# Attention in turns of four units: second pair's exponential bank by bank, and a first pair of banks that stays in place

## The chip, the core and the metric

The kernel runs on one core of one Trainium2 chip. The metric is the device time in microseconds (us). Before the change it is 1071.54 us, the median of 3 runs (1071.03 to 1071.62).

## What is computed

One token sequence of 2048 rows with 448 features goes through two blocks, and a sigmoid gate mixes their results. Everything is float32.

```python
g = sigmoid((x * gate_w).sum(-1, keepdims=True))
a = attention(x, wqkv, wo)        # 16 heads of 28, softmax over 2048 keys
b = mlp(layernorm(x), w1, b1, w2, b2)   # 448 -> 1792 (gelu) -> 448
return g * a + (1 - g) * b
```

The softmax subtracts the maximum of each row of the scores. The kernel gets it by a pass of its own: TensorE multiplies q and k once more, VectorE reduces each result to its maximum.

## The kernel before, in words

The kernel has two stages. In the first (to about 449.6 us) the projections and the MLP run, from an order that a planner made with costs in Python. In the second, which the change is in, attention runs in **turns** (`turn_of`, line 1147), one after another, with an order written out in the loop at line 1195.

The 16 heads form 4 groups of 4, and the queries 4 blocks of 512, so there are 16 rounds. A round has 64 **units**: a unit is the score block of one head, 128 keys by 512 queries, and needs one PSUM bank (128 partitions x 512 float32). `score` (line 1132) makes it in three matmuls, parts 0, 1 and 2, of which each uses one strip of 32 rows of TensorE; head j sits in strip j, and four strips work side by side. `soften` (line 1141) takes the exponential on ScalarE from PSUM into an SBUF tile (`p0` for the first pair, `p1` for the second). `batch` (line 1185) multiplies the four exponentials of a turn with the values, in 4 matmuls over 128 rows that add up in bank 7 (`pv`).

A turn of four units goes so: units 0 and 1 are the **first pair** (strips 0 and 1), units 2 and 3 the **second pair** (strips 2 and 3). TensorE's queue holds, in this order, a row-maximum matmul for strip 2 or 3 into bank 6 (`lone(behind, 6, turn)`, called L-behind below), the first pair's part 0, its part 1 with the second pair's part 0, its part 2 with the second pair's part 1, the second pair's part 2, then a row-maximum matmul for strip 0 or 1 (`lone(ahead, spare, turn)`, called L-ahead) and the four value matmuls of the turn before. ScalarE takes the first pair's exponential (both banks in one instruction, 128x1024) and then the second pair's (the same). VectorE reduces the results of L-behind and L-ahead (line 214, 128x512 to 128x1).

The banks: 0 to 5 form three pairs, (4,5), (2,3), (0,1), in this order in the list `pairs` (line 941 sorts them by the time at which the planner expects them free). A turn uses one for its first pair, one for its second, and the third is the **spare**, into whose first bank L-ahead writes. Line 1163 rotates them: a turn's spare is the next turn's first pair, and a turn's first pair is the next turn's second. So what stands in a bank must be gone before the next user writes: L-ahead waits for the exponential of the second pair of the turn before (the same banks), the next turn's first pair waits for VectorE's reduction of L-ahead, and the next turn's second pair waits for this turn's first exponential.

Row-maximum matmuls are left until about 978 us (`rowmax.left()`); then turns take seven units in banks 0 to 6, except near the output projections (`project`, line 1011, 12 matmuls through bank 6), where they stay at four.

Of the kernel before, what the change touches and what calls it, by code (L numbers as in the profile page):

```python
# [9 lines left out]
AF = mybir.ActivationFunctionType  # L10
# [19 lines left out]
SCALE = DH ** -0.5  # L30
# [5 lines left out]
def kernel(ctx: ExitStack, tc: tile.TileContext, xt, wqk, wv, wo, xk, w1, b1, w2, b2,  # L36
                          ident_d, sel_d, out):
    nc = tc.nc
# [35 lines left out]
    bk = banks.tile([P, 8, CH], F32, name="bk")  # L74
# [162 lines left out]
    rowmax = RowMax()  # L237
# [671 lines left out]
    for b, m in enumerate((0, 3, 4)):  # L909
        x = QK(0, m)  # L910
# [30 lines left out]
    pairs = sorted((0, 2, 4), key=lambda b: max(strips.free[b], strips.free[b + 1]))  # L941
# [134 lines left out]
    def begun(n, turn):  # L1076

        g, c = divmod(n, NC)
        if n + 1 < NG * NC:
            for j in range(4):  # L1080
                at(turn + 1 + j // 2, lambda j=j: fetch_qq(n + 1, j))
            at(turn + 7, lambda: split_qq(n + 1))
            at(turn + 10, lambda: load_ms(n + 1))
        if c == (0 if g == 0 else 2) and g < NG - 1:
            for j in range(4):
                at(turn + 2 + j, lambda j=j: fetch_kk(g + 1, j))
                at(turn + 10 + 2 * j, lambda j=j: split_kk(g + 1, j))
            at(turn + 18, lambda: key_row(g + 1))
            for t in range(2):
                at(turn + 12 + t, lambda t=t: load_v(g + 1, slice(8 * t, 8 * t + 8)))  # L1090
        if g == NG - 1:
            for i in range(TPC):
                at(turn + (8 if rowmax.left() else 7) + i, lambda i=i: fetch_acc(c, i))
                at(turn + (10 if rowmax.left() else 9) + i // 2, lambda i=i: weigh_acc(c, i))
            for x in range(NG - 1):
                at(turn + 4 + 2 * x, lambda x=x: split_o(x, c, ot[x][:, c * CH:(c + 1) * CH]))
# [21 lines left out]
    def lone(strips, b, turn):  # L1118
        s = min((s for s in strips if rowmax.ready(s) and turn >= cold[s]), key=lambda s: rowmax.cnt[s], default=None)
        if s is None:  # L1120
            return
        for kind, n, j in rowmax.one(s, bk[:, b]):
            if kind == "q":
                at(turn + 1, lambda n=n, j=j: rowmax.load_q(n, j))
            elif kind == "k":
                at(turn + 1, lambda n=n, j=j: rowmax.load_k(n, j))
                cold[j] = turn + 7
            else:
                at(turn + 1, lambda n=n: rowmax.close(n))
                at(turn + 2, lambda n=n: rowmax.store(n))  # L1130

    def score(x, p, b):
        n, k = divmod(x, 64)
        k, j = divmod(k, 4)
        r = slice(32 * j, 32 * j + DH + (p == 0))
        ks = slice(k * P, (k + 1) * P)
        w = (khi, klo, khi)[p][n // NC]
        q = (qh, qh, ql)[p][n % 3]
        nc.tensor.matmul(bk[:, b], w[r, ks], q[r], start=(p == 0), stop=(p == 2), skip_group_check=True)  # L1139

    def soften(u, half, b, count):
        t = ap.tile([P, 4 - half, CH], F32, name=f"p{half}")
        nc.scalar.activation(t[:, :count], bk[:, b:b + count], AF.Exp, scale=SCALE)  # L1143
        for i in range(count):
            prob[u + i] = t[:, i]

    def turn_of(u, turn):

        left = UNITS - u
        size = min(left, 7 if not rowmax.left() and not (tail and tail[0][0] <= turn + 1) else 4)  # L1150
        for x in range(u, u + size):
            n = x // 64
            if n not in begins:
                begins.add(n)
                begun(n, turn)
        if size > 4:
            for half, first, count in ((0, 0, 4), (1, 4, size - 4)):
                for p in range(3):
                    for i in range(first, first + count):
                        score(u + i, p, i)  # L1160
                soften(u + first, half, first, count)
            return size
        first, second, spare = (pairs[(2 * turn + i) % 3] for i in (0, 1, 2))
        na = min(size, 2)
        nb = size - na
        ahead = [(u + i) % 4 for i in range(2)]
        behind = [(u + i) % 4 for i in range(2, 4)]
        if rowmax.left() and turn not in projected:
            lone(behind, 6, turn)
        for step in range(4):  # L1170
            for i in range(na):
                if step < 3:
                    score(u + i, step, first + i)
            for i in range(nb):
                if step > 0:
                    score(u + 2 + i, step - 1, second + i)
            if step == 2:
                soften(u, 0, first, na)
        if nb:
            soften(u + 2, 1, second, nb)  # L1180
        if rowmax.left():
            lone(ahead, spare, turn)
        return size
# [11 lines left out]
    u = b = turn = 0  # L1195
    begun_half = False
    while b < UNITS // 4:
        before, quota = u, 99
        if u < UNITS:
            u += turn_of(u, turn)  # L1200
            if u - before > 5:
                quota = 3 + (before // 4 - b > 2)
                quota += 2 * (NT - b % NT) - begun_half == quota + 1
        for fn in agenda.pop(turn, ()):
            fn()
        if turn == 0:
            idle(6, 7)
        if before == UNITS:
            products(bk[:, 3, :D], (NC - 1) * TPC, range(NG - 1))
            before = u = UNITS  # L1210
        while 4 * b + 4 <= before and quota:
            if quota == 1 and not begun_half:
                if b % NT:
                    batch(b, turn, slice(0, CH // 2))
                    begun_half = True
                break
            last = batch(b, turn, slice(CH // 2 if begun_half else 0, CH))
            quota -= 1 if begun_half else 2
            b, begun_half = b + 1, False
            if last:  # L1220
                break
        if tail and tail[0][0] <= turn:
            project(tail.pop(0)[1])
            projected.add(turn + 1)
        turn += 1
# [53 lines left out]
```

## Time and profile before

| what | value |
|---|---|
| median of 3 runs | 1071.54 us |
| the profiled execution | 1071.13 us, of which the span from first to last instruction is 1069.3 us |
| TensorE busy | 1058.5 us (99%) |
| ScalarE busy | 647.6 us (61%) |
| VectorE busy | 749.8 us (70%) |
| GpSimd busy | 368.9 us (34%) |
| mean granted TensorE clock | 0.999 |

PE is TensorE's matmuls, PEld its weight loads (a matmul's waits stand at its weight load), ACT is ScalarE, DVE VectorE, POOL GpSimd, SP the engine that issues most DMAs. A row of the timeline has the start in us, the time from the first start to the last end of the merged instructions, engine, line, operation, result and operands, count, and in brackets how long the engine had been idle and what released it.

### The profile page before, as it was taken

The numbers are of one execution on the slowest core, as the hardware profiler recorded it, in microseconds if no ns is written. First come the engines' busy times: TensorE is split into PE (matmuls) and PEld (weight loads), VectorE is DVE, ScalarE is ACT, GpSimd is POOL, SyncE is SP. The second block draws the span as 40 slices with busy tenths as digits, with TensorE's granted clock in tenths as the row PEclk, the third lists the DMA queues.
The fourth block names the chain that finished last, engine by engine and source line by source line (L and its number), as shares of the span: only waits on it lengthen the run. The fifth ranks groups of instructions, "written<-read, shape, count | busy, mean of one in ns | idle before, by whom it ended". The sixth has DMA issues, their size and how long they took to land. (4 is left out here: it accounts for less than half of the span.)

```text
span 1069.3 us, 30804 instructions
## 1 busy us (share of the span) xinstructions
PE 1058.5 (99%) x13202; PEld 713.8 (67%) x13202; DVE 749.8 (70%) x1182; ACT 647.6 (61%) x773; POOL 368.9 (34%) x392
## 2 busy tenths in 40 slices
PE   9999999999999999999999999999999999999997
PEld 7999999999999999844444444444444444455455
DVE  4899998999999999866666665466666666634102
ACT  5234364033043033288888888888888888857762
POOL 5565578335344036451011101310111125363432
PEclk9999999999999999999999999999999999999999
DMA  7696443212100105230101101400002102121111
GB/s 236 217 272 216 169 106 97 86 55 61 38 13 10 37 16 124 75 90 22 30 2 23 28 13 31 116 22 17 15 21 64 51 12 55 29 62 47 45 54 61
DMA packets 47785, 73.18 MB, mean 68 GB/s; under 512 B 13840, under 2 KB 28816, under 8 KB 46848
## 3 DMA queue, kind: packets, MB, share of 16 engines
q1 hardware_dynamic: 33888, 39.11, 13.4%
q0 software_dynamic: 5120, 16.89, 5.8%
q10 hardware_dynamic: 8640, 15.21, 3.9%
q8 instruction: 103, 1.69, 0.7%
q14 instruction: 34, 0.28, 0.1%
HBM read 51.75 MB, written 19.31 MB: 66 GB/s over the span
## 5 line engine op out<-in xcount | busy, mean ns | idle before, releaser
L214 DVE TENSOR_REDUCE mx<-bk 128x1 f32<-128x512 f32 x1024 | 683.9, 690 | 209.6 <-PE bk L212 194.6
L1143 ACT ACTIVATE p<-bk 128x1024 f32<-128x1024 f32 (+1 forms) x500 | 495.1, 1043 | 106.0 <-PE bk L1139 106.0
L212 PE MATMUL bk<-kd,qd 28*128 28x512 f32 x1024 | 453.9, 444 | 0.0
L212 PEld LDWEIGHTS bk<-kd,qd 28*128 28x128 f32 x1024 | 185.9, 182 | 216.1 <-DVE mx L214 168.0
L488 PE MATMUL bk<-yh,w1f 32*128 32x512 f32 x1568 | 191.8, 393 | 0.0
L488 PE MATMUL bk<-yl,w1f 32*128 32x512 f32 x784 | 167.0, 391 | 0.0
L488 PEld LDWEIGHTS bk<-yh,w1f 32*128 32x128 f32 x1568 | 154.1, 183 | 1.3
L488 PE MATMUL bk<-w2h,hh 32*128 32x448 f32 x896 | 145.3, 366 | 1.0 <-issue 1.0
L488 PE MATMUL bk<-w2l,hh 32*128 32x448 f32 x896 | 144.2, 363 | 0.0
L1041 POOL TENSOR_TENSOR ot<-ob,rc 128x512 f32<-128x512 f32 x12 | 15.4, 1286 | 368.2 <-DMA rc<-rls 334.8
L1188 PE MATMUL bk<-p,va 128*32 128x512 f32 x1024 | 136.4, 605 | 0.0
L1188 PE MATMUL bk<-p,vb 128*32 128x512 f32 (+1 forms) x1056 | 135.2, 591 | 0.0
L363 POOL TENSOR_TENSOR hl<-h,hh 128x512 fp32r<-128x512 f32 x56 | 72.5, 1308 | 135.1 <-ACT hh L356 94.1
L488 PEld LDWEIGHTS bk<-yl,w1f 32*128 32x128 f32 x784 | 106.1, 183 | 0.2
L488 PEld LDWEIGHTS bk<-w2h,hh 32*128 32x128 f32 x896 | 102.8, 183 | 1.9 <-issue 1.4
L488 PEld LDWEIGHTS bk<-w2l,hh 32*128 32x128 f32 x896 | 102.6, 183 | 0.3
L488 PE MATMUL bk<-w2h,hl 32*128 32x448 f32 x896 | 93.5, 363 | 0.0
L1139 PE MATMUL bk<-yh,ka 29*128 29x512 f32 x512 | 93.0, 470 | 0.0
L1139 PE MATMUL bk<-yh,kb 29*128 29x512 f32 x512 | 87.2, 475 | 1.4 <-ACT p L1143 1.3
L398 ACT ACTIVATE gb<-bk 128x448 f32<-128x448 f32 x8 | 4.4, 545 | 131.0 <-PE bk L488 131.0
L355 ACT ACTIVATE h<-bk,b1s 128x512 f32<-128x512 f32 x56 | 38.3, 684 | 73.6 <-PE bk L488 65.4
L488 PEld LDWEIGHTS bk<-w2h,hl 32*128 32x128 f32 x896 | 82.3, 183 | 0.3
(141 smaller groups left out, 1636.0 us busy)
## 6 DMA issues: line engine op xcount, KB each, us to landing
qk<-qo ACTq DMA_DIRECT2D x28, 256.0 KB
raw<-in_xt SPq DMA_DIRECT2D x17, 256.0 KB
vs<-vt ACTq DMA_DIRECT2D x16, 256.0 KB
rc<-rls SPq DMA_DIRECT2D x60, 64.0 KB
bxr<-in_xk POOLq DMA_DIRECT2D x8, 448.0 KB, 5.9
acc<-gbs SPq DMA_DIRECT2D x16, 224.0 KB
out_y<-acc SPq DMA_DIRECT2D x16, 224.0 KB
qd<-qk SPq DMA_DIRECT2D x60, 56.0 KB
```

The lines of the kernel that those rows point to most:

```text
L212: nc.tensor.matmul(ps, self.qd[n % 2][r, i * P:(i + 1) * P], self.kd[r, k * 512:(k + 1) * 512], start=True, stop=True)
L214: nc.vector.reduce_max(self.mx[n % 2][:, j, i, k:k + 1], ps, axis=AX)
L355: nc.scalar.activation(h, bk[:, self.bank], AF.Gelu_apprx_tanh, bias=b1s[:, f:f + 1])
L363: nc.gpsimd.tensor_sub(hl[f], h, hh[f].bitcast(F32))
L398: nc.scalar.activation(gb, bk[:, self.bank, :D], AF.Copy)
L488: mm = nc.tensor.matmul(bk[:, x.bank, :n], a, b, start=x.first, stop=(len(x.rem) == 1 and m == len(ops) - 1), skip_group_check=True)
L1041: nc.gpsimd.tensor_mul(ot[g][:, c * CH:(c + 1) * CH], ob, rc)
L1139: nc.tensor.matmul(bk[:, b], w[r, ks], q[r], start=(p == 0), stop=(p == 2), skip_group_check=True)
L1143: nc.scalar.activation(t[:, :count], bk[:, b:b + count], AF.Exp, scale=SCALE)
L1188: nc.tensor.matmul(bk[32 * j:32 * j + 32, 7, sl], vg[n // NC][:, k, 32 * j:32 * j + 32], prob[4 * b + j][:, sl], start=(k == 0), stop=(k = ...
```

## The change

Two things change. `soften` gets a `step`: a count of banks for each ScalarE instruction. The first pair keeps one instruction of 128x1024; the second pair gets two of 128x512, one for each bank, while row-maximum matmuls are left. And the pairs no longer rotate: the first pair of units is always in `pairs[0]` (banks 4 and 5), the second pair alternates between `pairs[2]` and `pairs[1]`, and the spare is the other of these two.

```diff
-    def soften(u, half, b, count):
+    def soften(u, half, b, count, step=4):
         t = ap.tile([P, 4 - half, CH], F32, name=f"p{half}")
-        nc.scalar.activation(t[:, :count], bk[:, b:b + count], AF.Exp, scale=SCALE)
+        for i in range(0, count, step):
+            e = min(i + step, count)
+            nc.scalar.activation(t[:, i:e], bk[:, b + i:b + e], AF.Exp, scale=SCALE)
...
-        first, second, spare = (pairs[(2 * turn + i) % 3] for i in (0, 1, 2))
+        first, second, spare = (pairs[x] for x in ((0, 1, 2) if turn % 2 else (0, 2, 1)))
...
         if nb:
-            soften(u + 2, 1, second, nb)
+            soften(u + 2, 1, second, nb, 1 if rowmax.left() else 2)
```

TensorE's queue, one turn early in attention, before the change. L212 is the row-maximum matmul, L1139 the score matmuls (`ka` parts 0, `la` parts 1, `yl` parts 2), L1188 the value matmuls; the brackets name the engines whose signals an instruction waits for.

```order
L212 MATMUL bk<-kd,qd_153 128x512 [waits DVE_49]
L1139 MATMUL bk<-yh,ka 128x512 [waits DVE_49]
L1139 MATMUL bk<-yh,ka 128x512
L1139 MATMUL bk<-yh,la 128x512 x2
L1139 MATMUL bk<-yh,ka 128x512 [waits Activation_49]
L1139 MATMUL bk<-yh,ka 128x512
L1139 MATMUL bk<-yl,ka 128x512 x2
L1139 MATMUL bk<-yh,la 128x512 x2
L1139 MATMUL bk<-yl,ka 128x512 x2
L212 MATMUL bk<-kd,qd_153 128x512 [waits Activation_49]
L1188 MATMUL bk<-p_9911,va 32x512 x2
L1188 MATMUL bk<-p_9915,va 32x512 x2
```

The same turn after the change (line 1188 is now line 1190).

```order
L212 MATMUL bk<-kd,qd_153 128x512 [waits DVE_49]
L1139 MATMUL bk<-yh,ka 128x512 [waits Activation_49]
L1139 MATMUL bk<-yh,ka 128x512
L1139 MATMUL bk<-yh,la 128x512 x2
L1139 MATMUL bk<-yh,ka 128x512 [waits DVE_49]
L1139 MATMUL bk<-yh,ka 128x512
L1139 MATMUL bk<-yl,ka 128x512 x2
L1139 MATMUL bk<-yh,la 128x512 x2
L1139 MATMUL bk<-yl,ka 128x512 x2
L212 MATMUL bk<-kd,qd_153 128x512 [waits Activation_49]
L1190 MATMUL bk<-p_9915,va 32x512 x2
L1190 MATMUL bk<-p_9919,va 32x512
L1190 MATMUL bk<-p_9919,va 32x512 [waits Activation_49]
```

No matmul moved. The first pair's part 0 now waits for ScalarE and the second pair's part 0 for VectorE, where it was the other way round, and the fourth value matmul has a wait for ScalarE of its own, behind that of L-ahead.

ScalarE's queue in two turns before the change (p0 and p1 are the tiles of the first and second pair).

```order
L1143 ACTIVATE p_9883<-bk 128x1024 [waits PE_49,Activation_49]
L1143 ACTIVATE p_9887<-bk 128x1024 [waits PE_49,Activation_49]
L1143 ACTIVATE p_9911<-bk 128x1024 [waits PE_49,Activation_49]
L1143 ACTIVATE p_9915<-bk 128x1024 [waits PE_49,Activation_49]
```

And after it.

```order
L1145 ACTIVATE p_9886<-bk 128x1024 [waits PE_49,Activation_49]
L1145 ACTIVATE p_9890<-bk 128x512 [waits PE_49,Activation_49]
L1145 ACTIVATE p_9890<-bk 128x512 [waits PE_49]
L1145 ACTIVATE p_9915<-bk 128x1024 [waits PE_49,Activation_49]
L1145 ACTIVATE p_9919<-bk 128x512 [waits PE_49,Activation_49]
L1145 ACTIVATE p_9919<-bk 128x512 [waits PE_49]
```

Each second exponential has become two, and the first one keeps its size.

## The prediction

> **What bounds the kernel now.** First the page: which engine is busy where.
>
> ```profile
> span 1069.3 us, 30804 instructions
> PE 1058.5 (99%) x13202; PEld 713.8 (67%) x13202; DVE 749.8 (70%) x1182; ACT 647.6 (61%) x773; POOL 368.9 (34%) x392
> ```
>
> PE is busy throughout, but a matmul that fills up slowly counts as busy, so this row can't tell whether PE waits. The waits view can, in part: these three rows are the waits of L-ahead and L-behind for ScalarE and VectorE, and ScalarE's wait for scores (us in total, times, longest).
>
> ```profile
> PEld bk L212 <- DVE mx L214: 168.0, 204, 0.8
> ACT p L1143 <- PE bk L1139: 106.0, 244, 2.9
> PEld bk L212 <- ACT p L1143: 11.5, 67, 0.3
> ...
> ```
>
> The 168 us are no loss: they are weight loads of the next turn, which stand idle while PE runs the value matmuls. Only the timeline of single turns shows what matters. PEld's rows of two turns:
>
> ```profile
> 458.65 0.18 PEld L212 LDWEIGHTS bk<-kd,qd 28*128 28x128 f32 x1 [0.84 <-DVE mx L214]
> ...
> 459.58 0.18 PEld L212 LDWEIGHTS bk<-kd,qd 28*128 28x128 f32 x1 [0.17 <-ACT p L1143]
> 460.01 0.16 PEld L1188 LDWEIGHTS bk<-p,va 128*32 128x32 f32 x8 [0.25 <-issue]
> 461.01 0.18 PEld L212 LDWEIGHTS bk<-kd,qd 28*128 28x128 f32 x1 [0.84 <-DVE mx L214]
> ...
> 461.72 0.18 PEld L212 LDWEIGHTS bk<-kd,qd 28*128 28x128 f32 x1
> 462.14 0.16 PEld L1188 LDWEIGHTS bk<-p,va 128*32 128x32 f32 x8 [0.24 <-issue]
> 463.14 0.18 PEld L212 LDWEIGHTS bk<-kd,qd 28*128 28x128 f32 x1 [0.84 <-DVE mx L214]
> ```
>
> Turns start at 458.65, 461.01 and 463.14: one lasts 2.36 us, the next 2.13. In the long turn L-ahead loads 0.93 after the start and the value matmuls begin at 1.36; in the short one at 0.71 and 1.13. ScalarE's pairs of exponentials in the same turns:
>
> ```profile
> 457.59 1.94 ACT L1143 ACTIVATE p<-bk 128x1024 f32<-128x1024 f32 x2 [0.41 <-PE bk L1139]
> 459.73 1.94 ACT L1143 ACTIVATE p<-bk 128x1024 f32<-128x1024 f32 x2 [0.19 <-PE bk L1139]
> 462.09 1.94 ACT L1143 ACTIVATE p<-bk 128x1024 f32<-128x1024 f32 x2 [0.42 <-PE bk L1139]
> ```
>
> The pair that began at 457.59 ends at 459.53, and L-ahead loads at 459.58; the next ends at 461.67, and L-ahead loads at 461.72. So L-ahead comes 0.05 us after the second exponential of the turn before, both times. This closes a loop over two turns: L-ahead to value matmuls 0.43 (460.01 - 459.58), to the next turn's start 1.00, to its first exponential 1.08 (462.09 - 461.01), both exponentials 1.94, release 0.05: 4.50 us for two turns, against the 4.49 from 458.65 to 463.14. That loop, of TensorE and ScalarE in turn, sets the pace; neither engine is full.
>
> How fast would PE be without this wait? In a stretch with no L-ahead, turns start here:
>
> ```profile
> 673.79 0.50 PE L212 MATMUL bk<-kd,qd 28*128 28x512 f32 x1
> ...
> 675.92 0.50 PE L212 MATMUL bk<-kd,qd 28*128 28x512 f32 x1
> ...
> 678.04 0.50 PE L212 MATMUL bk<-kd,qd 28*128 28x512 f32 x1
> ...
> 680.17 0.50 PE L212 MATMUL bk<-kd,qd 28*128 28x512 f32 x1
> ```
>
> That is 6.38 us for three, 2.127 each. The short turn of 2.13 has both row-maximum matmuls: L-ahead then runs beside the second pair in another strip and costs nothing. 2.13 is PE's own floor.
>
> How many turns? The value matmuls in the two stretches of plain turns of four (first start to the start of the turn behind the last; PE's count in brackets, 8 records a turn):
>
> ```profile
> 452.09:936.32 484.23, 230.06 (x1728) 33.98 (x1728) 1.00 0.15 37
> 955.38:977.87 22.49, 10.66 (x84) 1.57 (x80) 1.00 0.15 35
> ```
>
> 1728 / 8 = 216 turns in 484.23 us and 80 / 8 = 10 (by weight loads) in 22.49: 226 turns in 506.72 us, 2.242 each, clock 1.00 throughout.
>
> **The change part by part.** *L-ahead's wait.* It needs only the first half of the second exponential now. What does a half cost? Exponentials by size, and a ScalarE copy of 512 columns from PSUM:
>
> ```profile
> L1143 ACT ACTIVATE p<-bk 128x1024 f32<-128x1024 f32 x467 | 453.2, 1022 | 98.4 <-PE bk L1139 98.4
> L1143 ACT ACTIVATE p<-bk 128x2048 f32<-128x2048 f32 x8 | 15.0, 1880 | 4.4 <-PE bk L1139 4.4
> L1143 ACT ACTIVATE p<-bk 128x1536 f32<-128x1536 f32 x8 | 11.6, 1451 | 0.0
> L295 ACT ACTIVATE qo<-bk x28: 580/598/603, 12.7 to 91.7; 128x512 f32<-128x512 f32 x28
> ```
>
> Each 512 columns cost 0.43 (1880 - 1451, 1451 - 1022), so a half lasts 1022 - 429 = 0.59 us, as the copy does. Two whole ones take 1.94, not 2.04, so neighbours overlap by 0.10. Counted from a turn's start: first exponential 1.08 to 2.10, first half 2.00 to 2.59, second half 2.49 to 3.08. ScalarE works 0.06 longer a turn than before (3.02), and hides it: its next exponential is due at 2.15 + 1.08 = 3.23. L-ahead is free at 2.64, which is 0.49 into the next turn, where 0.71 cost nothing. This wait goes, and with it the long turn. The fourth value matmul's new wait (second half, 3.08 + 0.05 = 3.13, or 0.98 into the next turn) lies ahead of the value matmuls' start at 1.13: nothing.
>
> The Trainium skill (ScalarE: Activation LUTs, Rules for kernel authors) budgets some 0.3 us an ACTIVATE plus 0.83 ns an element. By that a half would take 0.72 and a whole one 1.15; the rows above (1.02, and 0.92 from start to start) are shorter, so I go by them.
>
> *The first pair stays.* Its part 0 waits for the exponential of the same banks one turn earlier. What is queued behind it is everything on PE: the other strips' scores, L-ahead, the value matmuls. From a turn's start to the first exponential 1.08, the exponential 1.02, release 0.05 (as for L-ahead): the next first pair can load at 2.15. PE gets there at 2.13. So this loop, now over one turn, is the next limit: 2.15 a turn, 0.02 above PE's floor.
>
> *VectorE's waits.* In the turn from 461.01 its two reductions end at 461.54 + 1.43 = 462.97:
>
> ```profile
> 461.54 1.43 DVE L214 TENSOR_REDUCE mx<-bk 128x1 f32<-128x512 f32 x2 [0.73 <-PE bk L212]
> ```
>
> That is 1.96 into the turn, 2.01 with the release. It held the next first pair (2.13), and now holds the second, which is queued behind it: nothing, with a little more room than before.
>
> *The sum for plain turns:* 226 x 2.15 = 485.9 against 506.72: 20.8 us less.
>
> *Turn 0* has its second pair in `pairs[2]`, banks 0 and 1, instead of (2,3). The MLP's last copy out of PSUM comes from bank 0:
>
> ```profile
> 449.37 0.55 ACT L398 ACTIVATE h<-bk 128x448 f32<-128x448 f32 x1 [0.46 <-ACT h L398]
> 449.58 0.20 PEld L1139 LDWEIGHTS bk<-yh,ka 29*128 29x128 f32 x4 [0.36 <-issue]
> ```
>
> It ends at 449.92, release 449.97, where the turn's loads ran at 449.58 without a wait: 0.4 us more. *After the last turn of seven* (banks 4 to 6 are freed last) before had the second pair in (4,5), now the first is there:
>
> ```profile
> 1025.74 0.18 PEld L1139 LDWEIGHTS bk<-yh,kb 29*128 29x128 f32 x2 [0.41 <-issue]
> ...
> 1026.62 0.18 PEld L1139 LDWEIGHTS bk<-yh,kb 29*128 29x128 f32 x2 [0.59 <-ACT p L1143]
> 1026.63 0.18 PEld L1139 LDWEIGHTS bk<-yl,kb 28*128 28x128 f32 x2
> ```
>
> The first pair's part 0 (1025.74) moves to 1026.62; its part 2, now at 1026.63, falls one or two steps later: 0.2 us. Turns with projections and of seven units wait for neither loop and stay.
>
> Together 20.8 - 0.6 = 20.2 us less: 1050.9 by the profiled execution (1071.13), 1051.3 by the median of the runs (1071.54), which is 0.4 above it.
>
> Bounds: if the first pair's loop hides under PE's floor, 226 x 2.127 = 480.7, so 26.0 - 0.6 = 25.4 less: 1046. The loop's three terms are read to 0.01 each; 2.18 instead of 2.15 gives 492.7, 14.0 - 0.6 = 13.4 less: 1058.
>
> **The rivals.** *ScalarE becomes the bound (slower).* If instructions did not overlap when halves are among them, a turn on ScalarE would be 1.02 + 0.59 + 0.59 and three releases of 0.05: 2.35. With the first pair bound to the exponential one turn back there is no slack left to take this up: 226 x 2.35 = 531.1, 24 us more, plus 0.6: 1096. It decides against the change from 2.24 a turn, when the two halves add 0.09 beyond ScalarE's 0.15 of room. Against it stand the 1.94 rows, in which neighbours with waits of their own overlap; for it, only that no exponential of 512 columns stands in this trace. By the skill's budget, named above, the turn would be 1.15 + 0.72 + 0.72 = 2.60. Chance 0.07.
>
> *L-ahead still waits for both halves (slower).* Then the old loop stays and has 0.06 more in it: 4.56 for two turns, 2.28 each, 8.6 more, plus 0.6: 1081. TensorE's queue speaks against it: the fourth value matmul waits for ScalarE after L-ahead has, which it need not if L-ahead had seen the second half. Chance 0.03.
>
> *The wait moves to the first pair at full size (no change).* From 2.242 a turn on, that is if the first pair loads 0.09 later than worked out, nothing is gained: 1072. Chance 0.04. Between (2.18 to 2.24, 1058 to 1069), where part of the wait returns, 0.08. The Trainium skill (Perfetto Trace Analysis, Optimizing Tensor Performance, Matmuls) asks that matmul groups rotate through banks so that evacuation overlaps the next group's matmuls; the change ends this for the first pair. Here the rows leave it the value matmuls as cover: from the exponential's start at 1.08 to the next load at 2.13 it lacks only 0.02.
>
> **How the numbers follow.** The forecast, 2.13 to 2.18 a turn, has 0.78. A measurement of this kernel can tell about 0.2% from no change, 2.1 us. Faster by more: 0.78 + 0.08 = 0.86; within: 0.04; slower: 0.07 + 0.03 = 0.10. The range for 8 in 10 is 1046 to 1060: the forecast's own bounds, 1046 to 1058, and a little of the case between.
>
> **What would show it.** In the changed kernel's timeline all plain turns should last about 2.15, with no alternation; L-ahead should load without a wait on ScalarE; the first pair's load should stand 0.05 behind the first exponential's end, as PEld's small wait on ACT at L1139; a half should last 0.59, and ScalarE's three instructions 2.0 together. Halves of 0.65 or more in a row, turns above 2.24, or L-ahead 0.05 behind the second half would make it wrong.

## The result and the profile after

The changed kernel takes 1052.07 us, the median of 4 runs (1051.79 to 1052.28), against 1071.32 for the kernel before (4 runs, 1071.03 to 1071.62): a ratio of 0.982 (95% interval 0.9803 to 0.9837), 19.3 us less. The forecast was 1051.3, with a range of 1046 to 1060. The profiled execution takes 1052.1, its span 1050.3, which is 19.0 less than before's 1069.3.

The page, its span and its first block (engine, busy us, share of the span, instructions):

```profile
span 1050.3 us, 31035 instructions
...
PE 1039.1 (99%) x13202; PEld 694.9 (66%) x13202; DVE 749.4 (71%) x1182; ACT 661.7 (63%) x1004; POOL 368.9 (35%) x392
```

ScalarE has 231 instructions more, one for each second pair that is now split, and 14.1 us more work; the kernel is shorter all the same. PE's 99% says as little as before.

The waits of the changed kernel (us in total, times, longest):

```profile
ACT p L1145 <- PE bk L1139: 45.2, 61, 2.8
PEld bk L1139 <- ACT p L1145: 13.9, 17, 1.3
```

L-ahead's wait for ScalarE is gone from this list, and ScalarE's own wait for scores has fallen from 106.0 to 45.2 us. The score matmuls' wait for ScalarE (17 times) is not the first pair's wait in plain turns: four of the 17 lie between 652.87 and 661.51, where no L-behind stands ahead of the first pair, and the others from 958.80 on. Before it was 10 times and 7.0 us, all behind 1001. In plain turns the first pair's wait is too short for a bracket, and only the starts show it. PEld's rows of two plain turns and the start of a third:

```profile
558.18 0.18 PEld L212 LDWEIGHTS bk<-kd,qd 28*128 28x128 f32 x1 [0.84 <-DVE mx L214]
558.20 0.27 PEld L1139 LDWEIGHTS bk<-yh,ka 29*128 29x128 f32 x4
...
558.78 0.18 PEld L212 LDWEIGHTS bk<-kd,qd 28*128 28x128 f32 x1
...
560.33 0.18 PEld L212 LDWEIGHTS bk<-kd,qd 28*128 28x128 f32 x1 [0.84 <-DVE mx L214]
560.35 0.27 PEld L1139 LDWEIGHTS bk<-yh,ka 29*128 29x128 f32 x4
...
560.93 0.18 PEld L212 LDWEIGHTS bk<-kd,qd 28*128 28x128 f32 x1
...
562.46 0.18 PEld L212 LDWEIGHTS bk<-kd,qd 28*128 28x128 f32 x1 [0.84 <-DVE lt L1030]
562.50 0.26 PEld L1139 LDWEIGHTS bk<-yh,ka 29*128 29x128 f32 x4
```

L-behind starts the turns at 558.18, 560.33 and 562.46: 2.15 and 2.13, where before 2.36 and 2.13 took turns. L-ahead (558.78, 560.93) follows 0.60 after the start in both, without a wait. The first pair's load stands 0.02 to 0.04 behind L-behind's; from one such load to the next it is 2.15 both times (558.20, 560.35, 562.50). ScalarE's row in the first of these turns:

```profile
559.28 2.00 ACT L1145 ACTIVATE p<-bk 128x1024 f32<-128x1024 f32 x3
```

The whole exponential and the two halves take 2.00 together, and the first one starts 1.10 after the turn's start at 558.18. It lasts 1.02 and ends at 560.30; the first pair of the next turn loads at 560.35, which is 0.05 later. This is the one-turn loop of the prediction: counted from the first pair's own load (558.20) it is 1.08 + 1.02 + 0.05 = 2.15. The second half ends at 561.28, and L-ahead has loaded at 560.93, so it did not wait for that half. The halves as a group (count, busy us, mean ns of one, idle time before them):

```profile
L1145 ACT ACTIVATE p<-bk 128x512 f32<-128x512 f32 x462 | 250.2, 600 | 0.0
```

A half lasts 0.60, and ScalarE never stands idle before one. The value matmuls in the two stretches of plain turns (stretch, us, PE and PEld busy with counts, clock, DMA share, GB/s):

```profile
452.24:918.19 465.95, 230.20 (x1728) 34.14 (x1728) 1.00 0.15 38
937.24:958.80 21.56, 10.68 (x84) 1.57 (x80) 1.00 0.13 34
```

The same 226 turns take 465.95 + 21.56 = 487.51 us, 2.157 each, where before they took 506.72. That is 19.2 less, and so the whole of the change.

### The profile page after: what moved, and what is told of

Read it like the earlier page. It is cut to its first block, busy times and chain, and to the rows that moved or that the text cites. A ratio compares the mean times of both kernels' runs of the same rounds, so it can differ in the third digit from the quotient of the medians.

```text
span 1050.3 us, 31035 instructions
## 1 busy us (share of the span) xinstructions
PE 1039.1 (99%) x13202; PEld 694.9 (66%) x13202; DVE 749.4 (71%) x1182; ACT 661.7 (63%) x1004; POOL 368.9 (35%) x392
## 5 line engine op out<-in xcount | busy, mean ns | idle before, releaser
L1145 ACT ACTIVATE p<-bk 128x1024 f32<-128x1024 f32 (+1 forms) x731 | 509.5, 770 | 72.8 <-PE bk L1139 45.2
L212 PE MATMUL bk<-kd,qd 28*128 28x512 f32 x1024 | 439.1, 429 | 0.0
L212 PEld LDWEIGHTS bk<-kd,qd 28*128 28x128 f32 x1024 | 186.2, 182 | 198.4 <-DVE mx L214 166.3
L1139 PE MATMUL bk<-yh,ka 29*128 29x512 f32 x512 | 89.3, 469 | 0.0
L1139 PE MATMUL bk<-yh,kb 29*128 29x512 f32 x512 | 83.3, 474 | 2.3 <-ACT p L1145 2.1
```

What stands on the lines that cost most here:

```text
L212: nc.tensor.matmul(ps, self.qd[n % 2][r, i * P:(i + 1) * P], self.kd[r, k * 512:(k + 1) * 512], start=True, stop=True)
L1145: nc.scalar.activation(t[:, i:e], bk[:, b + i:b + e], AF.Exp, scale=SCALE)
```

## The experiments

The theory: before, L-ahead waited for the whole second exponential, and this closed a loop of 4.50 us over two turns; the split opens it, and then the first pair's loop over one turn (2.15) sets the pace, just above PE's floor of 2.13. Rivals: the order of the banks brings the gain and the split is beside the point; ScalarE's work sets the pace after the change; or there is no bound left, PE alone is. Each experiment below is compared with the kernel before on the same chip, by the ratio; the time of a plain turn is the stretch of its first 216 turns in the windows view, divided by 216.

**The new order of banks alone.** The kernel before, with one line changed:

```diff
-        first, second, spare = (pairs[(2 * turn + i) % 3] for i in (0, 1, 2))
+        first, second, spare = (pairs[x] for x in ((0, 1, 2) if turn % 2 else (0, 2, 1)))
```

> The banks in the new order, the second pair's exponential in one instruction as before. Theory (the gain comes from freeing the spare bank one half earlier; the order of banks alone frees nothing): L-ahead still waits for the whole second exponential of the turn before, the loop over two turns stays at 4.50 us, plain turns alternate between about 2.13 and 2.36, time 1071 to 1073 us. Rival (the gain comes from the order of banks): turns of about 2.15 without alternation, time 1050 to 1054 us.

Measured: 1071.69 us (10 runs), ratio 1.0006 (0.9997 to 1.0016). Its stretch, and PEld's rows at the starts of three turns and at L-ahead:

```profile
452.14:936.72 484.58, 230.06 (x1728) 33.99 (x1728) 1.00 0.14 36
```

```profile
559.80 0.18 PEld L212 LDWEIGHTS bk<-kd,qd 28*128 28x128 f32 x1 [0.84 <-DVE mx L214]
...
560.77 0.18 PEld L212 LDWEIGHTS bk<-kd,qd 28*128 28x128 f32 x1 [0.20 <-ACT p L1143]
...
562.19 0.18 PEld L212 LDWEIGHTS bk<-kd,qd 28*128 28x128 f32 x1 [0.84 <-DVE mx L214]
...
564.33 0.18 PEld L212 LDWEIGHTS bk<-kd,qd 28*128 28x128 f32 x1 [0.84 <-DVE mx L214]
```

These turns last 2.39 and 2.14, and in the long one L-ahead waits for ScalarE. The alternation is not everywhere in this run: turns that start at 470.04, 472.28 and 474.53 last about 2.25 each. What stays is the sum of two, since the mean is 2.243 (484.58 / 216), as before: the old loop, untouched. The order brings nothing by itself, so the first rival falls.

**The split alone.** The changed kernel, with the old rotation:

```diff
-        first, second, spare = (pairs[x] for x in ((0, 1, 2) if turn % 2 else (0, 2, 1)))
+        first, second, spare = (pairs[(2 * turn + i) % 3] for i in (0, 1, 2))
```

> The second pair's exponential bank by bank, the banks rotating as before. Theory: L-ahead's wait is gone, and no loop over one turn takes its place: the first pair waits for VectorE (2.01 us into the turn), the second for the first exponential (2.15, but it starts behind the first pair and one strip of it behind L-behind). Turns at TensorE's floor of 2.13, 226 x 2.127 = 480.7 us, so 1046 to 1048 us: some 5 us faster than the changed kernel. Rival (the order of banks is needed, the first pair's wait for VectorE or the second's for ScalarE takes back what the halves gain): 1052 us or more, at worst the 1071 of before.

Measured: 1046.82 us (1046.40 to 1048.41), ratio 0.9774 (0.976 to 0.9789), whose interval lies wholly below that of the change.

```profile
452.38:913.26 460.88, 230.23 (x1728) 34.13 (x1728) 1.00 0.14 39
```

```profile
561.23 0.18 PEld L212 LDWEIGHTS bk<-kd,qd 28*128 28x128 f32 x1 [0.84 <-DVE lt L1030]
...
563.35 0.18 PEld L212 LDWEIGHTS bk<-kd,qd 28*128 28x128 f32 x1 [0.84 <-DVE mx L214]
563.36 0.29 PEld L1139 LDWEIGHTS bk<-yh,ka 29*128 29x128 f32 x4
...
565.49 0.18 PEld L212 LDWEIGHTS bk<-kd,qd 28*128 28x128 f32 x1 [0.84 <-DVE mx L214]
```

Turns of 2.12 and 2.14, mean 2.134: PE's floor, with the first pair's load beside L-behind's. The split is the whole gain, and the fixed first pair takes about 5 us of it back (1052.07 - 1046.82 = 5.25), as its loop says: 226 x (2.157 - 2.134) = 5.2. The Trainium skill (Perfetto Trace Analysis, Optimizing Tensor Performance, Matmuls) asks that matmul groups rotate through banks so that evacuation overlaps the next group's matmuls; here the two kernels differ by that rotation alone, and it is worth these 5 us.

**The first pair bank by bank too.** The changed kernel with

```diff
-                soften(u, 0, first, na)
+                soften(u, 0, first, na, 1 if rowmax.left() else 2)
```

> The changed kernel with the first pair's exponential bank by bank too (two instructions of 128x512 instead of one of 128x1024). Theory (the first pair's loop counts, unit by unit): unit 0 may load 1.08 + 0.59 + 0.05 = 1.72 us into the turn, which is never late, unit 1 only at 1.08 + 0.48 + 0.61 + 0.05 = 2.22, later than the 2.15 of both today. That costs 0.09 in turns whose L-ahead is in unit 1's strip, nothing in the others: 2.17 a turn on average, some 1055 us (1050 to 1062). Rival (finer exponentials free banks sooner and that always helps): TensorE's floor of 2.13, 1047 us.

Measured: 1052.91 us (1052.68 to 1053.28), ratio 0.9832 (0.9816 to 0.9849): not to be told from the change, whose interval it overlaps.

```profile
452.93:919.33 466.40, 230.12 (x1728) 34.12 (x1728) 1.00 0.14 38
```

```profile
519.80 0.18 PEld L212 LDWEIGHTS bk<-kd,qd 28*128 28x128 f32 x1 [0.84 <-DVE mx L214]
...
520.38 0.18 PEld L212 LDWEIGHTS bk<-kd,qd 28*128 28x128 f32 x1
...
521.92 0.18 PEld L212 LDWEIGHTS bk<-kd,qd 28*128 28x128 f32 x1 [0.84 <-DVE mx L214]
...
522.57 0.18 PEld L212 LDWEIGHTS bk<-kd,qd 28*128 28x128 f32 x1
...
524.12 0.18 PEld L212 LDWEIGHTS bk<-kd,qd 28*128 28x128 f32 x1 [0.84 <-DVE mx L214]
```

The mean is 2.159, but now from turns of 2.12 and 2.20. L-ahead stands 0.58 after the start of the short one (520.38 - 519.80) and 0.65 after that of the long one (522.57 - 521.92), so the 0.07 is lost among the scores ahead of it: by the trace unit 1's load, whose bank a second half frees now, comes at 522.00, which is 0.07 after unit 0's and 0.05 after that half's end (521.95). The cost has moved within the pair and has not gone. Four halves a turn on ScalarE make nothing slower, which speaks against ScalarE as the bound.

**More work on ScalarE, in the loop and beside it.** If the first pair's loop is the limit, 128 columns more behind the first exponential, reading its bank, must cost their whole time, and the same work behind the second half nothing. If ScalarE's sum of work is the limit, both cost the same. The first kernel writes the extra result into a part of the tile that nothing uses:

```diff
+        if again:
+            nc.scalar.activation(t[:, 2, 0:P], bk[:, b, 0:P], AF.Exp, scale=SCALE)
...
-                soften(u, 0, first, na)
+                soften(u, 0, first, na, again=rowmax.left())
```

> The changed kernel with an additional ScalarE instruction directly behind the first exponential, which reads the first 128 columns of the first bank once more, but writes into an unused part of the tile, so that it needn't wait for the end of the instruction ahead (the earlier one did: 0.03 us after the end, then 0.28 us). Theory (first pair's loop): it ends about 0.17 to 0.18 us after the exponential, the loop is longer by that: 2.33 a turn, 226 x 0.175 = 40 us more, 1088 to 1095 us. Rival (something else sets the pace and 0.15 us of ScalarE fit in): at most 1057 us.

The second does so in the second pair, with `bk[:, b + 1, 0:P]` as its input:

```diff
-            soften(u + 2, 1, second, nb, 1 if rowmax.left() else 2)
+            soften(u + 2, 1, second, nb, 1 if rowmax.left() else 2, again=rowmax.left())
```

> The same additional instruction (128 columns, into an unused part of the tile), behind the second pair's second half, which lies off the first pair's loop. ScalarE's turn is then 0.90 + 0.48 + 0.49 + 0.17 = 2.04 us, less than 2.15. Theory: no more than 1 us, 1051 to 1054 us. Rival (ScalarE's total work sets the pace): as much as with the instruction in the loop, some 1091 us.

Measured: in the loop 1088.81 us (1087.80 to 1090.53), ratio 1.0169 (1.0149 to 1.0189); beside it 1052.20 (1050.73 to 1052.61), ratio 0.9821 (0.98 to 0.9841), the same as the change. The stretch of the first:

```profile
451.84:952.54 500.70, 230.29 (x1728) 34.20 (x1728) 1.00 0.14 35
```

And of the second:

```profile
453.79:918.72 464.93, 230.21 (x1728) 34.13 (x1728) 1.00 0.15 38
```

The turns last 2.318 and 2.152. ScalarE's rows of the first kernel, and PEld's loads behind them:

```profile
556.10 2.26 ACT L1145 ACTIVATE p<-bk 128x512 f32<-128x512 f32 x3
558.26 0.27 ACT L1147 ACTIVATE p<-bk 128x128 f32<-128x128 f32 x1
558.41 2.26 ACT L1145 ACTIVATE p<-bk 128x512 f32<-128x512 f32 x3
```

```profile
558.38 0.18 PEld L212 LDWEIGHTS bk<-kd,qd 28*128 28x128 f32 x1 [0.84 <-DVE mx L214]
558.58 0.20 PEld L1139 LDWEIGHTS bk<-yh,ka 29*128 29x128 f32 x4
```

The first exponential ends at 558.36 (556.10 + 2.26), the extra instruction at 558.53, and the first pair loads at 558.58, 0.20 behind L-behind where it was 0.02. So the extra instruction lengthens the loop by 0.17, to 2.32, and the turn grows by 0.16. On ScalarE it puts off the next start by 0.15 (558.41 - 558.26). The same work beside the loop costs nothing: ScalarE's sum is not the bound.

**The same two, written onto the same place.** An earlier form of this pair repeats 128 columns of the exponential itself, first in the first pair (`t[:, 0, 0:P], bk[:, b, 0:P]`), then in the second half (`t[:, 1, 0:P], bk[:, b + 1, 0:P]`); the calls are changed as above.

> The changed kernel with one more ScalarE instruction a turn, of 128 columns, directly behind the first exponential: it repeats the first 128 columns of the first bank, so it also lies between the first exponential and the next first pair. Theory (the first pair's loop sets 2.15 a turn): the loop is longer by the whole instruction, about 0.16 us from start to start: 2.31 to 2.33 a turn, 226 x 0.16 = 36 us more, 1086 to 1092 us. Rival (TensorE's floor or something else sets the pace and ScalarE has room for 0.15 us): at most 1056 us.

> The changed kernel with the same additional ScalarE instruction of 128 columns, but behind the second pair's second half, repeating the first 128 columns of that bank. ScalarE's work a turn is that of the kernel with the repeat behind the first exponential. Theory (only the first pair's loop counts, ScalarE's work elsewhere fits into its 0.15 us of room): 1052 to 1056 us. Rival (ScalarE's total work sets the pace): as much as with the repeat behind the first exponential, some 1088 us.

Measured: 1107.74 us (1106.77 to 1108.93), ratio 1.0344 (1.0326 to 1.0362), and 1063.41 (1061.85 to 1064.23), ratio 0.9925 (0.9909 to 0.994). The order between the two is as expected, both sizes are missed. ScalarE's rows of the second:

```profile
584.10 2.00 ACT L1145 ACTIVATE p<-bk 128x1024 f32<-128x1024 f32 x3
586.13 0.28 ACT L1147 ACTIVATE p<-bk 128x128 f32<-128x128 f32 x1
586.30 2.00 ACT L1145 ACTIVATE p<-bk 128x1024 f32<-128x1024 f32 x3
```

The three exponentials that begin at 584.10 end at 586.10, and the repeat begins at 586.13. Since it writes what its predecessor wrote, it waits for that one's end and loses the overlap: 0.03 + 0.28 by these rows, where in the loop above it was 0.15. In the first of these two kernels the same 0.31 stands in the loop; its first exponential starts 1.02 after the pair's load by the trace, not 1.08, since the repeat has taken over one of its waits (see the next experiment). That gives 1.02 + 1.02 + 0.31 + 0.05 = 2.40 a turn, and 2.40 is the median of that trace. In the second kernel ScalarE works without a pause but its wait for itself, 586.30 - 584.10 = 2.20 a turn: here ScalarE is the bound, which the change itself never comes to. So this pair by itself would not have told the theories apart; the two runs before do.

**One wait less on the first exponential.** In the changed kernel each first exponential and each first half waits for two engines, TensorE and ScalarE itself. A one-column instruction behind the second half (its result goes unused) takes the second of these waits over:

```diff
+        if again:
+            nc.scalar.activation(t[:, 2, 0:1], t[:, 1, 0:1], AF.Exp, scale=SCALE)
```

It is called in the second pair, as above. ScalarE's queue in the changed kernel:

```
L1145 ACTIVATE p_13194<-bk 128x1024 [waits PE_49,Activation_49]
L1145 ACTIVATE p_13198<-bk 128x512 [waits PE_49,Activation_49]
L1145 ACTIVATE p_13198<-bk 128x512 [waits PE_49]
```

And with the one column:

```
L1145 ACTIVATE p_13296<-bk 128x1024 [waits PE_49]
L1145 ACTIVATE p_13300<-bk 128x512 [waits PE_49] x2
L1147 ACTIVATE p_13300<-p_13300 128x1 [waits Activation_49]
```

> The changed kernel with an additional ScalarE instruction of one column behind the second pair's second half: it reads that half's result in SBUF, so it waits for ScalarE's own signal, and the next first exponential needn't wait for one any more (one wait instead of two). With the repeat behind the first exponential such an exponential with one wait began 0.06 us earlier. Theory (the first pair's loop of 2.15 is the limit, and 0.06 of it is this second wait): the loop falls to 2.09, below TensorE's floor, ScalarE's turn is 0.90 + 0.48 + 0.62 + 0.03 + 0.07 = 2.10; turns of 2.13, 1046 to 1049 us, so the kernel with an instruction more is faster. Rival (the second wait costs nothing, or the loop isn't the limit): 1052 to 1056 us.

Measured: 1045.45 us (1044.04 to 1046.08), ratio 0.976 (0.9742 to 0.9778). More work, and by the two ratios (0.982 - 0.976) 0.6% less time than the change.

```profile
452.27:912.52 460.25, 230.07 (x1728) 33.99 (x1728) 1.00 0.14 38
```

ScalarE's rows, and PEld's start of a turn:

```profile
559.71 0.20 ACT L1147 ACTIVATE p<-p 128x1 f32<-128x1 f32 x1
559.82 1.98 ACT L1145 ACTIVATE p<-bk 128x1024 f32<-128x1024 f32 x3
```

```profile
558.78 0.18 PEld L212 LDWEIGHTS bk<-kd,qd 28*128 28x128 f32 x1 [0.84 <-DVE mx L214]
558.78 0.29 PEld L1139 LDWEIGHTS bk<-yh,ka 29*128 29x128 f32 x4
```

The first exponential starts 1.04 after the first pair's load (559.82 - 558.78), where it was 1.08 (559.28 - 558.20). So the second wait is worth 0.04, not the 0.06 that was expected, and the loop is 1.04 + 1.02 + 0.05 = 2.11, below PE's floor all the same; the turn is 2.131, and the first pair loads beside L-behind. The loop has been shortened without touching banks or split, and the time followed it down to the floor and no further.

Could any small instruction at this place do the same? The kernel with 128 columns more beside the loop has one there, and is no faster than the change. The difference between the two is in ScalarE's sequencer, which waits for the additional signal in an instruction of its own. Its rows at the exponentials, in the kernel with 128 columns and in the one with one column (count, shortest, median and longest in ns, first and last start):

```profile
L1145 ACTq EVENT_SEMAPHORE  x496: 17/17/799, 452.0 to 1030.6; - x166
...
L1145 ACTq EVENT_SEMAPHORE  x35: 17/17/790, 450.5 to 1024.1; - x35
```

The 496, as many as in the changed kernel, have become 35. So an instruction at this place does not help by itself; what the faster kernel has beyond it is the wait that is gone.

**Both cures together.** The last kernel with the old rotation:

> Both at once: the second pair bank by bank, the banks rotating as before the change, and the instruction of one column that saves the first exponential's second wait. Theory (each of the two alone already has turns at TensorE's floor of 2.13): nothing is left to gain in the turns; without the changed kernel's 0.3 us in the first turn 1044.5 to 1047 us. Rival (the two gains add up, some 5 us each): 1041 us or less.

Measured: 1045.97 us (1045.13 to 1046.82), ratio 0.9764 (0.9748 to 0.9781). The two don't add, as each alone already reaches PE's floor. These three (the split with the old rotation, and the two with the one-column instruction) beat both kernels of the change; their intervals overlap, and the plainest of them is the split with the old rotation.

## Why the prediction was right, point by point

*The bound before, and L-ahead's wait.* Right. Without the split the loop over two turns stays whatever the order of the banks (2.243 a turn), and with it the loop is gone under both orders.

*The halves.* Right: 0.60 for 0.59, and 2.00 for 2.0 for the three. The rival of a ScalarE that no longer overlaps (2.35 a turn) is refuted by the 2.00 and by the extra work that cost nothing beside the loop. The rival that L-ahead waits for both halves is refuted by L-ahead's place, 0.60 after the start and ahead of the second half's end, and the rival without a change by the time. The prediction set the rows against a budget of the Trainium skill by which a half would take 0.72. The measured 0.60 is nearer to another sentence of that page (ScalarE: Activation LUTs, What ACT_TABLE_LOAD costs): 0.186 us + 0.833 ns an element without a pointer operand, and an overlap of some 0.093 between neighbours. That gives, as an estimate worked out from that page, 0.61 for a half and 2.08 for the three.

*The first pair's loop.* Right as a mechanism, and the experiments in and beside it show it: 0.17 more in it costs 0.16 a turn, 0.04 less brings the turn to PE's floor. Its size was right too: from one first pair's load to the next, the median of the first stretch is 2.15 by the trace. But the sum took every turn at 2.15, and the mean is 2.157, so 19.2 us less in place of 20.8. This is the largest miss of the sum. Late turns account for it: those above 2.16 exceed 2.15 by some 1.6 us in all. The longest comes with a late first exponential, here on PEld:

```profile
499.76 0.18 PEld L212 LDWEIGHTS bk<-kd,qd 28*128 28x128 f32 x1 [0.84 <-DVE mx L214]
...
501.92 0.18 PEld L212 LDWEIGHTS bk<-kd,qd 28*128 28x128 f32 x1 [0.84 <-DVE mx L214]
502.23 0.20 PEld L1139 LDWEIGHTS bk<-yh,ka 29*128 29x128 f32 x4
```

and on ScalarE:

```profile
501.16 2.00 ACT L1145 ACTIVATE p<-bk 128x1024 f32<-128x1024 f32 x3 [0.44 <-PE bk L212]
```

It starts 1.40 after its turn's start in place of 1.10, ends at 502.18, and the next first pair loads at 502.23, 0.31 late. A loop with no slack hands every such delay on to the end; why this exponential was late was not tried.

*Turn 0.* Right in direction and nearly in size. PEld's rows:

```profile
449.39 0.18 PEld L1139 LDWEIGHTS bk<-yh,ka 29*128 29x128 f32 x2 [0.36 <-issue]
...
449.76 0.18 PEld L1139 LDWEIGHTS bk<-yh,ka 29*128 29x128 f32 x2
...
452.24 0.18 PEld L212 LDWEIGHTS bk<-kd,qd 28*128 28x128 f32 x1 [0.36 <-issue]
```

The two pairs' part 0, before one row of four at 449.58, now are two rows 0.37 apart. The turn takes 452.24 - 449.39 = 2.85 against 452.09 - 449.58 = 2.51 before: 0.34 more, where 0.4 was said. That the attention began 0.19 earlier (449.39 against 449.58) was in no part of the sum; it happens to cover some of the miss above.

*After the last turn of seven.* Mis-sized: 0.2 was said, and next to nothing was lost. PEld's rows:

```profile
1007.59 0.20 PEld L1139 LDWEIGHTS bk<-yh,kb 29*128 29x128 f32 x4 [1.31 <-ACT p L1145]
1007.70 0.20 PEld L1139 LDWEIGHTS bk<-yh,lb 28*128 28x128 f32 x4
1007.93 0.20 PEld L1139 LDWEIGHTS bk<-yl,kb 28*128 28x128 f32 x4
```

The first pair does wait for the seven's exponential. But then all four units start together and need three steps, where two pairs one behind the other need four: the late pair catches up beside the other. From the last value weights ahead of this turn to the first behind it, it is 2.35 us (1006.15 to 1008.50 by the trace), where it was 2.32 (1025.20 to 1027.52): 0.03 more. The step that failed was "its part 2 falls one or two steps later".

*What the prediction did not ask.* It took the two edits as one. It named the fixed first pair's lack of 0.02 as a price within the gain, but not that the old rotation with the split would have no such price.

## What to carry to other kernels

When one engine reads 99% busy, take the starts of single turns and add up the chain from one start to the next, over two turns if they alternate: the chain that sums to the period is the bound. To open it, release first what is needed first (here one bank of two, by splitting the instruction that empties it), and then work out the next-longest chain, since the gain ends there. An edit that comes with another should be costed alone: here one of the two took a fifth of the other's gain back.

## What the runs showed of the hardware beyond this

A second wait on a ScalarE instruction costs about 0.04 us here: the first exponential starts 1.08 after the first pair's load with two waits and 1.04 with one, even though another instruction was added to get there. (From the turn's start it is 1.10 and 1.04, but 0.02 of that is the first pair's late load.) In the trace the second wait is an instruction of ScalarE's sequencer of its own, and some 460 of these are gone in the faster kernel (35 in place of 496, two a turn). The instruction that took the wait over, of one column, lasts 0.20, but the next starts 0.11 after it (559.82 - 559.71). A ScalarE instruction that waits for its predecessor's end starts 0.03 behind it and lasts 0.28 for 128 columns; one that needn't wait puts off the next start by 0.15.
